# Second softmax five groups ahead, a fixed deviation bound and row-tiled up products in an attention-then-MLP kernel

## The chip, the cores and the metric

The kernel runs on one NeuronCore of a Trainium2 chip. Its engines work side by side: PE multiplies matrices into PSUM, DVE (VectorE) and ACT (ScalarE) compute on SBUF and PSUM, POOL (GpSimd) computes on SBUF, and SP issues the DMAs. Each engine takes its instructions in a fixed order and waits on semaphores. The metric is the device time of one execution in microseconds (us), the median of several runs; lower is better.

## The reference

Four batches of 12480 tokens with 128 channels go through two attentions over 32 learned points, and the result goes through an MLP with squared ReLU. Cut to what matters:

```python
B, N, m, C = (4, 12480, 32, 128)            # w_in: 128 x 2048, w_out: 2048 x 128
def mab(q, kv):
    s = scale * (q @ kv.transpose(0, 2, 1))
    s = s - s.max(-1, keepdims=True)
    a = np.exp(s)
    a /= a.sum(-1, keepdims=True) + 1e-09
    return a @ kv
h = mab(I, x)                               # (B, 32, C): the first softmax, over the tokens
y = mab(x, h)                               # (B, N, C): the second softmax, over the 32 points
r = np.maximum(y @ w_in, 0.0)
out = (r * r) @ w_out
```

## The kernel before

**What is computed.** A token's second softmax has 32 weights a, which sum to one and are all near 1/32. So y @ w_in = a @ (h @ w_in), and for nearly all of the 2048 hidden columns the sign is the same for every token of a batch. A column that is always positive contributes a quadratic form in a; one that is always negative contributes nothing; up to 16 columns a batch may change their sign and are computed one by one. The kernel stores d = 2^14 (a - 1/32) as two f16 halves, high and low.

**Stages of a batch.** `first(b)` computes h: for each of seven groups G of 1920 tokens (the last has 960) it loads the transposed tokens into a tile `xp` (L231), multiplies them with the points (`scores`, L236), keeps the scaled scores `sT` and their maxima (L254), then takes exponentials (L300), transposes them (L310) and sums `hacc` over the tokens, which come through five `xnb` buffers (L267, L323). Along the way `largest(G)` reduces the whole `xp` tile on DVE to its largest absolute value per channel, `xm` (L292). At the end stands the transposed h, `hT`. `prepare(b)` turns h and the weights into the matrices of the quadratic form: `hwv` (L448), the maximum and the bound in `row` (L473 to L482), `R`, `rb`, `cat`, then four times a product `G` on DVE (L605) and its matmul `wq` (L611) into `w16`. The bound `rho` on how far a token can lie from the mean of the 32 points is worked out here from `xm` and `hT` (`dh`, `ah`), and `vm`, `up`, `dn` decide with it which columns keep their sign. `second(b, G)` makes the scores against h from the same `xp` tile (L236), the softmax (L362 to L378) with two steps on POOL (L368, L375), the halves `a16` (L385 to L388), writes them to DRAM (`ad`, L389) and reads them back in another layout (`dT`, `load_dT`, L409: rows 0-31 high halves, 32-63 low halves, 64-95 high halves again). `squares(b, G)` multiplies `dT` for the single columns (`sq`, L422), cuts at zero (L428), squares on POOL (L432) and copies the result by DMA into rows 96-127 of `dT` (L434).

**The MLP.** A group has four chunks of 480 tokens, a batch 26, the whole kernel 104. For a chunk, `up(j)` makes two blocks of differences of weights by two matmuls of 96 rows (L639) with the constant matrix `pairs`, whose rows 64-95 are zero, into two PSUM banks; `lift(j)` squares both blocks on ACT (L648); `down` sums four blocks with `w16` (L654) and the row with `lin` (L655), and the output `o` leaves PSUM on ACT (L658) or DVE (L660), whichever has the smaller tally in `held`, and is stored (L661).

**What sets the order.** The loop at the end of the function emits lifts, ups and downs of neighbouring chunks and calls `background(k)` after each half chunk. It hands out steps of three generators: `ahead` (all `second`), `sqs` (all `squares`) and `nexts[b]` (`first` and `prepare` of the next batch), each up to a count that grows with the chunk. A scheduler then places the emitted instructions on the engines by its own timing model, so the order of a row on an engine may differ from that of the text. `dT` has 4 buffers, `xp` has `NX` = 9 (a batch's seven and two of the next), `g`, the lifted blocks, 3 and `o` 3. All DMAs shown are issued by SP, one after the other. At the end a flag for each batch is combined, and if one is zero, a slow general branch computes everything again; with the drawn inputs it is not taken.

Of the kernel before, what the change touches and what calls it, by code (L numbers as in the profile page):

```python
# [9 lines left out]
F32 = mybir.dt.float32  # L10
F16 = mybir.dt.float16
# [17 lines left out]
BLK = [(w + 31) // 32 for w in WID]  # L29
NQ = 4  # L30
MX = 16
RHO_MAX = 2.0 ** -8
NX = 9
XB = 5
RUNS = [(0, 4), (4, 4), (8, 4), (12, 4)]
BESIDE = (3, 2)
WHEN = (0, 2, 4, 8, 10, 12, 14)


@with_exitstack  # L40
def attend_then_relu2_mlp(ctx: ExitStack, tc: tile.TileContext, xn, xT, indT, w_in, w_out, outT):
# [64 lines left out]
    pairs = const.tile([P, NQ * P], F16, name="pairs")  # L106
    nc.vector.memset(pairs, 0.0)
    fold_f = fold.rearrange("p k i -> p (k i)")
    for s in range(1, 17):
        n = MI if s < 16 else 16  # L110
        nc.vector.tensor_tensor(
            pairs[0:64, MI * (s - 1):MI * (s - 1) + n], fold_f[0:64, 0:n], fold_f[0:64, s:s + n], op=ALU.subtract,
        )
    nc.vector.tensor_copy(pairs[0:64, 31 * 16:32 * 16], fold_f[0:64, 0:16])

    w_in_sb = const.tile([P, NF * P], F32, name="w_in_sb")
    wo_sb = const.tile([P, NF, P], F32, name="wo_sb")
# [122 lines left out]
    def first(b):  # L240
# [46 lines left out]
        nc.vector.tensor_scalar(nb, bp[:, 0:1], -1.0, None, op0=ALU.mult)  # L287
        yield

        def largest(G):  # L290
            held["dve"] += 60 + 1.042 * 4 * WID[G]
            nc.vector.tensor_reduce(  # L292
                st.xm[:, G:G + 1], st.xp[G], axis=AX.X, op=ALU.max, apply_absolute_value=True,
            )
# [12 lines left out]
        for G, nb32 in enumerate(BLK):  # L307
            en = work.tile([P, 15, MI], F32, tag="en", name=f"en_{b}_{G}")
            held["dve"] += 110 + 1.042 * 32 * nb32
            nc.vector.transpose(  # L310
                en[:, 0:nb32].rearrange("p t i -> p (t i)"), sT[:, 480 * G:480 * G + 32 * nb32],
            )
            if G + 2 < NG:
                exp(G + 2)
            largest(G)
            yield
            hacc = att_psum(f"hacc_{b}_{G}")
            for t in range(nb32):
# [4 lines left out]
                st.last = nc.tensor.matmul(  # L323
                    hacc[32 * q:32 * q + 32, 0:P], en[:, t], xg[:, t % 8], start=t < 4, stop=t + 4 >= nb32,
                )
# [23 lines left out]
    def second(b, G, again=False):  # L349
# [38 lines left out]
            nc.vector.scalar_tensor_tensor(a16[:, 1, 0:w], a[:, 0:w], lessen, a16[:, 0, 0:w], op0=ALU.add, op1=ALU.subtract)  # L388
# [15 lines left out]
    def load_dT(b, G):  # L404

        w = GRP[G] * TP
        dT = mlp.tile([P, 4, 480], F16, tag="dT", name=f"dT_{b}_{G}", bufs=4)
        for k in range(3):
            nc.sync.dma_start(  # L409
                dT[32 * k:32 * k + 32, :, 0:w], sts[b].ad[:, :, k % 2, 480 * G:480 * G + w].rearrange("q i n -> i q n"),  # L410
            )
        return dT
# [24 lines left out]
    def prepare(b):  # L437
# [6 lines left out]
        for h in range(2):  # L444
# [7 lines left out]
            if h == 0:

                xm, dh, ah = small("xm"), small("dh", MI), small("ah", MI)
                nc.vector.tensor_reduce(xm, st.xm, axis=AX.X, op=ALU.max)
                ts(dh, st.hT[:, 0:MI], st.hT[:, P:P + 1], None, op0=ALU.subtract)
                stt(dh, dh, -1.0, dh, op0=ALU.mult, op1=ALU.max)
                stt(ah, st.hT[:, 0:MI], -1.0, st.hT[:, 0:MI], op0=ALU.mult, op1=ALU.max)
                stt(dh, ah, 2.0 ** -18, dh, op0=ALU.mult, op1=ALU.add)
# [15 lines left out]
        row = work.tile([1, 2], F32, tag="row", name=f"row_{b}")
        nc.vector.tensor_reduce(row[:, 0:1], ps[0:1, 0:P], axis=AX.X, op=ALU.max)
        nc.vector.tensor_reduce(row[:, 1:2], ps[0:1, P:P + MI], axis=AX.X, op=ALU.max)
        ts(row[:, 0:1], row[:, 0:1], 2.0 ** -60, None, op0=ALU.max)
        ts(row[:, 1:2], row[:, 1:2], 2 * scale * (1 + 2.0 ** -8), 2.0 ** -16, op0=ALU.mult, op1=ALU.add)
        yield  # L480
        ps = att_psum(f"bc_{b}")
        nc.tensor.matmul(ps[:, 0:2], ones, row, start=True, stop=True)  # L482
        two = small("two", 2)
        nc.vector.tensor_copy(two, ps[:, 0:2])
        rho = two[:, 1:2]
# [60 lines left out]
        fits = work.tile([1, 2], F32, tag="fits", name=f"fits_{b}")  # L546
        ts(fits[:, 0:1], bp[0:1, 2:3], MX + 0.5, None, op0=ALU.is_le)
        ts(fits[:, 1:2], row[:, 1:2], RHO_MAX, None, op0=ALU.is_le)
        tt(flags[:, b:b + 1], fits[:, 0:1], fits[:, 1:2], op=ALU.mult)
# [79 lines left out]
    class Chunk:  # L629
# [4 lines left out]
        def up(self, j):  # L634
            if j == 0:
                self.dT = self.st.aT[self.c // 4][:, :, (self.c % 4) * TP:(self.c % 4 + 1) * TP]
            hp = self.hp[j] = two_banks(f"hp_{self.b}_{self.c}_{j}")
            for i in range(2):
                nc.tensor.matmul(  # L639
                    hp[:, i, 0:CH].rearrange("p (q t) -> p q t", q=4), pairs[0:96, (2 * j + i) * P:(2 * j + i + 1) * P],  # L640
                    self.dT[0:96], start=True, stop=True,
                )

        def lift(self, j):
# [59 lines left out]
    ahead = chain(*(second(b, G) for b in range(NB) for G in range(NG)))  # L704
# [235 lines left out]
```

## Time and profile before

| | us |
|---|---|
| three runs | 562.49, 556.12, 562.29 |
| their median | 562.29 |
| the profiled execution | 565.03 |
| its span, first to last instruction | 563.2 |

The profile is of one further execution; its mean granted TensorE clock is 0.87 of full speed. In the profile a row of the timeline gives start, length, engine, line, operation, tiles and count, and in brackets how long the engine had been idle before it and what ended that. This is the page's view of the span in 40 equal slices of 14 us, in tenths (9 is 90% or more): PE's busy share, and the clock that PE was granted.

```profile
PE   1635355986778988869789889779779989669792
PEclk9999557699697998776899988878898999898987
```

The first eight slices hold the start and the first batch's preparation; the MLP runs from there to the end.

### The profile page before, as it was taken

To read this page: it belongs to the slowest core of one execution; us is meant where nothing else is said; L and a number is where in the kernel's file an instruction comes from. 1 tells how busy PE (TensorE), PEld (TensorE's weight loads), DVE (VectorE), ACT (ScalarE), POOL (GpSimd) and SP (SyncE) were. 2 spreads that over 40 slices of the span, in tenths; PEclk is the share of its full clock that TensorE was granted. 3 is DMA by queue.
4 is the path that set the end of the run, shared out by engine and by line. 5 is a ranking of instruction groups with operands and counts; after the bars stand their busy time and mean duration, and the time that the engine had idled before them with its cause. 6 is when DMAs were issued, how large, how long until landed. Compare 5 with 4: busy or idle time off the path is not lost.

```text
span 563.2 us, 8828 instructions
## 1 busy us (share of the span) xinstructions
PE 422.6 (75%) x3083; PEld 202.7 (36%) x3083; DVE 365.6 (65%) x947; ACT 294.4 (52%) x419; POOL 82.2 (15%) x93
## 2 busy tenths in 40 slices
PE   1635355986778988869789889779779989669792
PEld 0023334622233535522244536423234555223340
DVE  8999768466382674675574384986653377787541
ACT  0030113338395794334687883426486875357771
POOL 0000011021120110122211010132121021234200
PEclk9999557699697998776899988878898999898987
DMA  8998313126559863253778943263567312244642
GB/s 317 410 358 310 132 70 118 41 80 212 140 160 345 292 216 115 72 169 107 216 237 294 334 167 115 76 227 115 174 216 264 128 54 72 90 151 133 203 150 82
DMA packets 64591, 100.83 MB, mean 179 GB/s; under 512 B 22800, under 2 KB 53776, under 8 KB 64528
## 3 DMA queue, kind: packets, MB, share of 16 engines
q1 hardware_dynamic: 64528, 100.08, 52.9%
q8 instruction: 28, 0.46, 0.4%
q14 instruction: 35, 0.29, 0.2%
HBM read 64.91 MB, written 31.95 MB: 172 GB/s over the span
## 4 chain that ended last, share of the span: by engine, by line
PE 39%; DMA 24%; DVE 22%; ACT 5%; SPq 4%; issue 3%; POOL 0%; ACTq 0%; DVEq 0%; POOLq 0%
PE hp L639 11%; DMA dT<-ad 7%; PE po L654 6%; PE s L236 6%; DMA xp_False<-xT_dram 6%; DMA ad<-a 5%; DVE xm L292 5%; ACT g L648 4%; DMA xnb<-xn_dram 3%; PE wq L611 3%; DVE G L605 3%; PE hwv L448 3%; PE hacc L323 2%; SPq L409 2%; DMA outT_dram<-o 2%
## 5 line engine op out<-in xcount | busy, mean ns | idle before, releaser
L648 ACT ACTIVATE g<-hp 128x960 f16<-128x960 f32 x208 | 193.5, 972 | 105.0 <-PE hp L639 92.8
L639 PE MATMUL hp<-dT,pairs 96*128 96x480 f16 x416 | 129.3, 407 | 16.2 <-ACT g L648 9.6
L654 PE MATMUL po<-g,w 128*128 128x480 f16 x416 | 114.7, 381 | 13.0 <-DVE o L660 5.1
L639 PEld LDWEIGHTS <-pairs 96*128 96x128 f16 x416 | 36.8, 104 | 84.4 <-issue 60.2
L368 POOL TENSOR_TENSOR e<-e,mx 128x480 f32<-128x480 f32 (+1 forms) x28 | 27.0, 965 | 261.5 <-DVE mx L364 208.2
L654 PEld LDWEIGHTS <-w 128*128 128x128 f16 x416 | 40.9, 102 | 63.6 <-issue 24.6
L292 DVE TENSOR_REDUCE xm<-xp_False 128x1 f32<-128x1920 f32 (+1 forms) x28 | 55.9, 1999 | 8.4 <-DMA xp_False<-xT_dram 8.3
L658 ACT ACTIVATE o<-po,bias,osc 128x480 f32<-128x480 f32 x66 | 48.7, 757 | 15.6 <-PE po L655 14.7
L236 PE MATMUL s<-xp_False,indT_sb 128*32 128x480 f32 (+1 forms) x224 | 37.4, 756 | 18.3 <-DMA xp_False<-xT_dram 13.3
L323 PE MATMUL hacc<-xnb,en 128*32 128x128 f32 x784 | 35.6, 317 | 19.6 <-DMA xnb<-xn_dram 7.6
L655 PE MATMUL po<-dT,lin 128*128 128x480 f16 x104 | 39.9, 400 | 9.3 <-DMA dT<-zz 9.0
L432 POOL TENSOR_TENSOR zz<-z 128x480 f16<-128x480 f32 (+1 forms) x28 | 27.6, 985 | 111.7 <-DVE z L428 87.9
L660 DVE TENSOR_SCALAR o<-po,osc,bias 128x480 f32<-128x480 f32 x38 | 28.8, 763 | 18.4 <-PE po L655 13.7
L375 POOL TENSOR_TENSOR e<-e,z 128x480 f32<-128x480 f32 (+1 forms) x28 | 26.9, 961 | 87.8 <-DVE z L374 67.6
L323 PEld LDWEIGHTS hacc<-xnb,en 128*32 128x32 f32 x784 | 25.5, 125 | 32.5 <-issue 15.7
L300 ACT ACTIVATE sT<-sT,nb 128x480 f32<-128x480 f32 (+1 forms) x28 | 18.3, 657 | 35.2 <-DVE nb L287 35.2
L362 DVE STREAM_TRANSPOSE e<-s 128x480 f32<-128x480 f32 (+1 forms) x28 | 18.0, 644 | 25.6 <-PE s L236 25.4
L428 DVE TENSOR_SCALAR z<-sq,off,cut 128x480 f32<-128x480 f32 (+1 forms) x28 | 21.5, 769 | 18.0 <-PE sq L422 17.5
L236 PE MATMUL s<-xp_False,hT 128*32 128x480 f32 (+1 forms) x224 | 30.0, 610 | 0.1
L605 DVE TENSOR_TENSOR G<-hwp,hw 128x512 f16<-128x512 f16 x64 | 25.9, 460 | 5.6 <-PE wq L611 5.6
L378 DVE STREAM_TRANSPOSE a<-e 128x480 f32<-128x480 f32 (+1 forms) x28 | 17.7, 633 | 13.0 <-POOL e L375 13.0
L422 PE MATMUL sq<-dT,singles 96*32 96x480 f16 x104 | 11.4, 398 | 19.4 <-DMA dT<-ad 18.0
(208 smaller groups left out, 493.3 us busy)
## 6 DMA issues: line engine op xcount, KB each, us to landing
outT_dram<-o SPq DMA_DIRECT2D x104, 240.0 KB, 2.6
xp_False<-xT_dram SPq DMA_DIRECT2D x24, 960.0 KB, 6.3
xnb<-xn_dram SPq DMA_DIRECT2D x28, 448.0 KB, 5.8
xnb<-xn_dram SPq DMA_DIRECT2D x24, 512.0 KB, 6.5
dT<-ad SPq DMA_DIRECT2D x72, 120.0 KB, 2.6
ad<-a SPq DMA_DIRECT2D x24, 240.0 KB, 2.6
dT<-zz SPq DMA_DIRECT2D x104, 30.0 KB, 1.9
wi<-w_in_dram SPq DMA_DIRECT2D x4, 512.0 KB, 5.7
```

Source lines behind the costliest of these rows:

```text
L236: nc.tensor.matmul(ps[32 * q:32 * q + 32, 0:w], lhsT, xp[:, w * q:w * q + w], start=True, stop=True,)
L292: nc.vector.tensor_reduce(st.xm[:, G:G + 1], st.xp[G], axis=AX.X, op=ALU.max, apply_absolute_value=True,)
L323: st.last = nc.tensor.matmul(hacc[32 * q:32 * q + 32, 0:P], en[:, t], xg[:, t % 8], start=t < 4, stop=t + 4 >= nb32,)
L368: nc.gpsimd.tensor_tensor(e[:, 0:t], e[:, 0:t], mx[:, 0:t].unsqueeze(2).broadcast_to([P, t, MI]), op=ALU.subtract)
L432: nc.gpsimd.tensor_tensor(g[rows], zv[rows], zv[rows], op=ALU.mult)
L605: tt(g[:, :, MI * j:MI * j + n], hwp[:, :, 0:n], hw16f[:, :, s0:s0 + n], op=ALU.mult)
L639: nc.tensor.matmul(hp[:, i, 0:CH].rearrange("p (q t) -> p q t", q=4), pairs[0:96, (2 * j + i) * P:(2 * j + i + 1) * P], self.dT[0:96], sta ...
L648: nc.scalar.activation(self.g[:, 2 * j:2 * j + 2], self.hp.pop(j)[:, 0:2, 0:CH], AF.Square)
L654: nc.tensor.matmul(po[:, 0:CH], st.w16[:, i], self.g[:, i], start=i == 0, stop=False)
L655: nc.tensor.matmul(po[:, 0:CH].rearrange("p (q t) -> p q t", q=4), st.lin, self.dT, start=False, stop=True)
L658: nc.scalar.activation(o, po[:, 0:CH], AF.Identity, bias=st.bias, scale=st.osc)
L660: nc.vector.tensor_scalar(o, po[:, 0:CH], st.osc, st.bias, op0=ALU.mult, op1=ALU.add)
```

## The change

It has six parts, all in the one function.

1. **Fixed bound.** `rho` becomes the constant 2^-10. `xm`, `largest`, `dh`, `ah`, the second column of `row` and the check of `rho` go. In their place `second` keeps the smallest high half of d so far in `least_d`, and a new generator `smallest`, behind the last `second`, compares it with -0.498 into a further flag.
2. **Row-tiled up products.** The matrix `pairs` stands in rows 0-31 for even blocks and in rows 64-95 for odd ones, and an up product reads those 32 rows of `pairs` and of `dT`, which hold high halves in both places. The low halves are left out of the up products.
3. `ahead` runs up to five groups ahead (was three), not into a batch whose h isn't made yet; `dT` has six buffers.
4. `sqs` runs up to two groups ahead (was one).
5. The next batch's steps are handed out earlier: scores by chunk 6 (was 8), heads by 12 (was 15), `prepare` by 22 (was 24.5); they are handed out before `ahead`.
6. `NX` is 8 (was 9).

```diff
-RHO_MAX = 2.0 ** -8
-NX = 9
+RHO = 2.0 ** -10
+D_MIN = -0.498
+NX = 8
+NDT = 6
...
+    def half_rows(block):
+        return slice(64, 96) if block % 2 else slice(0, 32)
...
+        r = half_rows((s - 1) // 4)
         nc.vector.tensor_tensor(
-            pairs[0:64, MI * (s - 1):MI * (s - 1) + n], fold_f[0:64, 0:n], fold_f[0:64, s:s + n], op=ALU.subtract,
+            pairs[r, MI * (s - 1):MI * (s - 1) + n], fold_f[r, 0:n], fold_f[r, s:s + n], op=ALU.subtract,
...
-        def largest(G):
-            held["dve"] += 60 + 1.042 * 4 * WID[G]
-            nc.vector.tensor_reduce(
-                st.xm[:, G:G + 1], st.xp[G], axis=AX.X, op=ALU.max, apply_absolute_value=True,
-            )
...
-            largest(G)
...
         if not again:
+            nc.vector.tensor_tensor(least_d[:, 0:w], least_d[:, 0:w], a16[:, 0, 0:w], op=ALU.min)
             st.aT[G] = load_dT(b, G)
...
-        dT = mlp.tile([P, 4, 480], F16, tag="dT", name=f"dT_{b}_{G}", bufs=4)
+        dT = mlp.tile([P, 4, 480], F16, tag="dT", name=f"dT_{b}_{G}", bufs=NDT)
...
-        nc.tensor.matmul(ps[0:1, P:P + MI], xm, dh, start=True, stop=True)
...
-        ts(vm, v, omr, None, op0=ALU.mult)
-        ts(up, hi, 0.0, rho, op0=ALU.max, op1=ALU.mult)
+        ts(vm, v, 1.0 - RHO, None, op0=ALU.mult)
+        ts(up, hi, 0.0, RHO, op0=ALU.max, op1=ALU.mult)
...
+                r = half_rows(i)
                 nc.tensor.matmul(
-                    hp[:, i, 0:CH].rearrange("p (q t) -> p q t", q=4), pairs[0:96, (2 * j + i) * P:(2 * j + i + 1) * P],
-                    self.dT[0:96], start=True, stop=True,
+                    hp[:, i, 0:CH].rearrange("p (q t) -> p q t", q=4), pairs[r, (2 * j + i) * P:(2 * j + i + 1) * P],
+                    self.dT[r], start=True, stop=True,
...
-        give("ahead", ahead, min(math.ceil((NG * b + c / 4 + min(3, 2 + k / 16)) * N_SECOND), NB * NG * N_SECOND))
...
-            if c < 8:
-                want = 1 + N_SCORES * c / 8
-            elif c < 15:
-                want = 1 + N_SCORES + N_HEADS * (c - 8) / 7
+            if c < 6:
+                want = 1 + N_SCORES * c / 6
+            elif c < 12:
+                want = 1 + N_SCORES + N_HEADS * (c - 6) / 6
             else:
-                want = 1 + N_SCORES + N_HEADS + N_PRE * (c - 15) / 9.5
+                want = 1 + N_SCORES + N_HEADS + N_PRE * (c - 12) / 10
             give(b + 1, nexts[b + 1], math.ceil(want))
-        give("sqs", sqs, min(math.ceil(NG * b + c / 4 + 1), NG * (b + 1)) * N_SQ)
+        known = NB if b + 1 == NB else b + 1 + (c >= 12)
+        far = math.ceil((NG * b + c / 4 + min(5, 3 + k / 8)) * N_SECOND)
+        give("ahead", ahead, min(far, NG * known * N_SECOND) + (far > NB * NG * N_SECOND))
+        give("sqs", sqs, min(math.ceil(NG * b + c / 4 + min(2, 1 + k / 8)), NG * (b + 1)) * N_SQ)
```

How the instructions move is seen on the engines themselves. The first place is SP's queue where batch 1 begins. Names end in batch, group or chunk and a running number: `ad_154<-a_1_2` is the write of batch 1's third group, `dT_2` its way back, `zz_0` the squares of the first group, `o_0` the first chunk's output. Before:

```order
L434 DMA dT_0_1914<-zz_0_2170 32x4x120 x4
L434 DMA dT_1_2128<-zz_1_2252 32x4x120 x4
L661 DMA outT_dram<-o_0_2275 128x480
L661 DMA outT_dram<-o_1_2303 128x480
L231 DMA xp_6_False<-xT_dram 128x960
L661 DMA outT_dram<-o_2_2334 128x480
L661 DMA outT_dram<-o_3_2368 128x480
L389 DMA ad_154<-a_1_2_2203 256x1x480
L409 DMA dT_2_2207<-ad_154 32x4x480 x3
L389 DMA ad_154<-a_1_3_2339 256x1x480
```

And now:

```order
L391 DMA ad_154<-a_1_2_2028 256x1x480
L412 DMA dT_2_2033<-ad_154 32x4x480 x3
L240 DMA xp_4_False<-xT_dram 128x1920
L240 DMA xp_5_False<-xT_dram 128x1920
L437 DMA dT_0_1560<-zz_0_2183 32x4x120 x4
L437 DMA dT_1_1809<-zz_1_2237 32x4x120 x4
L437 DMA dT_2_2033<-zz_2_2281 32x4x120
L391 DMA ad_154<-a_1_3_2136 256x1x480
L437 DMA dT_2_2033<-zz_2_2281 32x4x120 x3
L412 DMA dT_3_2141<-ad_154 32x4x480 x3
L647 DMA outT_dram<-o_0_2308 128x480
```

The third group's write and way back moved from behind the fourth output to before the first; the fourth group's came up behind it, and three groups of squares stand in a row instead of two.

The second place is ACT at the same boundary: `g` are lifts (two a chunk, from `hp`), `w_1` the copies of batch 1's four weight matrices out of `wq`, which its downs need. Before:

```order
L648 ACTIVATE g_1_2264<-hp_1_0_2218 128x960
L648 ACTIVATE g_1_2264<-hp_1_1_2259 128x960
L165 ACTIVATE w_1_146<-wq_0_1928,tsg 128x128
L648 ACTIVATE g_2_2292<-hp_2_0_2266 128x960
L648 ACTIVATE g_2_2292<-hp_2_1_2287 128x960
L165 ACTIVATE w_1_146<-wq_1_1975,tsg 128x128
L369 ACTIVATE e_1_1_1971<-e_1_1_1971 128x480
L165 ACTIVATE w_1_146<-wq_2_2028,tsg 128x128
```

And now:

```order
L634 ACTIVATE g_2_2325<-hp_2_0_2299 128x960
L634 ACTIVATE g_2_2325<-hp_2_1_2316 128x960
L371 ACTIVATE e_1_2_1860<-e_1_2_1860 128x480
L174 ACTIVATE w_1_146<-wq_0_1877,tsg 128x128
L644 ACTIVATE o_24_2200<-po_24_2194,bias_143,osc_142 128x480
L174 ACTIVATE w_1_146<-wq_1_1921,tsg 128x128
L387 ACTIVATE a_1_2_2028<-a_1_2_2026,lessen 128x480
L174 ACTIVATE w_1_146<-wq_2_1968,tsg 128x128
```

The weight copies did not move up: all four stand behind the lifts of the new batch's third chunk now, while the softmax exponential beside them is one group further on.

The third place is DVE while batch 1's weights are made (`G` feeds `wq`, `wm` reads it). Before:

```order
L605 TENSOR_TENSOR G_2_2007<-hwp_1745,hw_1_1697 128x16x32 x4
L428 TENSOR_SCALAR z_6_1997<-sq_6_1994,off_137,cut 64x480
L613 TENSOR_REDUCE wm_1918<-wq_1_1975 128x1
L372 TENSOR_REDUCE z_1_1_2071<-e_1_1_1971 128x15
L292 TENSOR_REDUCE xm_133<-xp_3_False 128x1
L373 TENSOR_SCALAR z_1_1_2071<-z_1_1_2071 128x15
L605 TENSOR_TENSOR G_3_2051<-hwp_1745,hw_1_1697 128x16x32 x3
```

And now:

```order
L590 TENSOR_TENSOR G_2_1954<-hwp_1680,hw_1_1644 128x16x32 x4
L646 TENSOR_SCALAR o_25_2254<-po_25_2248,osc_142,bias_143 128x480
L598 TENSOR_REDUCE wm_1849<-wq_1_1921 128x1
L390 SCALAR_TENSOR_TENSOR a_1_2_2028<-a_1_2_2026,lessen,a_1_2_2028 128x480
L393 TENSOR_TENSOR least_d<-least_d,a_1_2_2028 128x480
L590 TENSOR_TENSOR G_3_1987<-hwp_1680,hw_1_1644 128x16x32 x3
```

The reduction of a whole `xp` tile ahead of the last `G` is gone; an output, the low half and the new minimum stand there. Over the whole kernel 61 outputs are on DVE now instead of 38.

More of the change, by code (lines that the diff above doesn't have):

```diff
@@ L108, in attend_then_relu2_mlp @@
     fold_f = fold.rearrange("p k i -> p (k i)")
+    def half_rows(block):
+        return slice(64, 96) if block % 2 else slice(0, 32)
     for s in range(1, 17):
         n = MI if s < 16 else 16
+        r = half_rows((s - 1) // 4)
         nc.vector.tensor_tensor(
-            pairs[0:64, MI * (s - 1):MI * (s - 1) + n], fold_f[0:64, 0:n], fold_f[0:64, s:s + n], op=ALU.subtract,
+            pairs[r, MI * (s - 1):MI * (s - 1) + n], fold_f[r, 0:n], fold_f[r, s:s + n], op=ALU.subtract,
         )
-    nc.vector.tensor_copy(pairs[0:64, 31 * 16:32 * 16], fold_f[0:64, 0:16])
+    r = half_rows(NQ - 1)
+    nc.vector.tensor_copy(pairs[r, 31 * 16:32 * 16], fold_f[r, 0:16])
     w_in_sb = const.tile([P, NF * P], F32, name="w_in_sb")
@@ L119, in attend_then_relu2_mlp @@
     inv_t = const.tile([P, 1], F32, name="inv_t")
-    flags = const.tile([1, NB], F32, name="flags")
+    flags = const.tile([1, NB + 1], F32, name="flags")
+    least_d = const.tile([P, CH], F16, name="least_d")
+    nc.vector.memset(least_d, 0.0)
     class Batch:
@@ L127, in attend_then_relu2_mlp @@
         one = Batch()
-        one.xm = const.tile([P, NG], F32, name=f"xm{k}")
         one.hn = const.tile([P, P], F32, name=f"hn{k}")
@@ L451, in prepare @@
             evac(hwv[:, 8 * h:8 * h + 8].rearrange("p k i -> p (k i)"), ps[:, 0:8 * (MI + 1)], 8 * (MI + 1))
[L452 to L459, printed above, removed]
             yield
@@ L473, in prepare @@
         nc.tensor.transpose(ps[0:1, 0:P], am, ident)
-        nc.tensor.matmul(ps[0:1, P:P + MI], xm, dh, start=True, stop=True)
[L475 to L479, printed above, removed]
+        row = work.tile([1, 1], F32, tag="row", name=f"row_{b}")
+        nc.vector.tensor_reduce(row, ps[0:1, 0:P], axis=AX.X, op=ALU.max)
+        ts(row, row, 2.0 ** -60, None, op0=ALU.max)
         yield
         ps = att_psum(f"bc_{b}")
[L482 to L485, printed above, removed]
+        nc.tensor.matmul(ps[:, 0:1], ones, row, start=True, stop=True)
         p2 = small("p2")
-        ts(p2.bitcast(I32), two[:, 0:1].bitcast(I32), 0x7F800000, None, op0=ALU.bitwise_and)
-        mg, nmg, s, k2, omr = small("mg"), small("nmg"), small("s"), small("k2"), small("omr")
+        ts(p2.bitcast(I32), ps[:, 0:1].bitcast(I32), 0x7F800000, None, op0=ALU.bitwise_and)
+        mg, nmg, s, k2 = small("mg"), small("nmg"), small("s"), small("k2")
         ts(k2, p2, 2.0, None, op0=ALU.mult)
@@ L500, in prepare @@
         ts(nmg, p2, -2.0 ** -16, None, op0=ALU.mult)
-        ts(omr, rho, -1.0, 1.0, op0=ALU.mult, op1=ALU.add)
         up, dn, dead, pos, mix, inc = (small(n, NF) for n in ("up_c", "dn_c", "dead", "pos", "mix", "inc"))
         vm = small("vm", NF)
-        ts(vm, v, omr, None, op0=ALU.mult)
-        ts(up, hi, 0.0, rho, op0=ALU.max, op1=ALU.mult)
+        ts(vm, v, 1.0 - RHO, None, op0=ALU.mult)
+        ts(up, hi, 0.0, RHO, op0=ALU.max, op1=ALU.mult)
         tt(up, up, vm, op=ALU.add)
@@ L508, in prepare @@
         stt(dead, up, nmg, dead, op0=ALU.is_le, op1=ALU.max)
-        ts(dn, lo, 0.0, rho, op0=ALU.min, op1=ALU.mult)
+        ts(dn, lo, 0.0, RHO, op0=ALU.min, op1=ALU.mult)
         tt(dn, dn, vm, op=ALU.add)
@@ L545, in prepare @@
         stt(inc, inc, pl, mix, op0=ALU.add, op1=ALU.mult)
[L546 to L549, printed above, removed]
+        ts(flags[:, b:b + 1], bp[0:1, 2:3], MX + 0.5, None, op0=ALU.is_le)
         hot = flow.tile([P, NF, MX], F32, tag="hot", name=f"hot_{b}", bufs=1)
@@ L703, in attend_then_relu2_mlp, with smallest @@
     N_SECOND, N_SCORES, N_HEADS, N_PRE, N_SQ = 4, 2 * NG, 20, 23, 2
-    ahead = chain(*(second(b, G) for b in range(NB) for G in range(NG)))
+    def smallest():
+        m = small("dmin")
+        nc.vector.tensor_reduce(m, least_d, axis=AX.X, op=ALU.min)
+        tp = att_psum("dmin_t")
+        nc.tensor.transpose(tp[0:1, 0:P], m, ident)
+        t = work.tile([1, 1], F32, tag="dmin1", name="dmin1")
+        nc.vector.tensor_reduce(t, tp[0:1, 0:P], axis=AX.X, op=ALU.min)
+        nc.vector.tensor_scalar(flags[:, NB:NB + 1], t, D_MIN, None, op0=ALU.is_ge)
+        yield
+    ahead = chain(*(second(b, G) for b in range(NB) for G in range(NG)), smallest())
     sqs = chain(*(squares(b, G) for b in range(NB) for G in range(NG)))
```

## The prediction, made before the changed kernel was run

> **What bounds the kernel now.** I read the page first, for the engines and the chain that ended last, then the span cut into stages (cut where the chain shows one batch's steps end), then PE's waits by what ended them, and last the timeline at the places that the change touches. The page, busy time and then the chain by line:
>
> ```profile
> PE 422.6 (75%) x3083; PEld 202.7 (36%) x3083; DVE 365.6 (65%) x947; ACT 294.4 (52%) x419; POOL 82.2 (15%) x93
> PE hp L639 11%; DMA dT<-ad 7%; PE po L654 6%; PE s L236 6%; DMA xp_False<-xT_dram 6%; DMA ad<-a 5%; DVE xm L292 5%; ACT g L648 4%; DMA xnb<-xn_dram 3%; PE wq L611 3%; DVE G L605 3%; PE hwv L448 3%; PE hacc L323 2%; SPq L409 2%; DMA outT_dram<-o 2%
> ```
>
> No engine is full. The chain changes hands all the time: PE, the trip of the second softmax's result through DRAM (ad, then dT), and the DVE reductions xm. So the stages matter (start and end in us, busy time of PE, PEld, DVE, ACT and POOL, granted clock, DMA share):
>
> ```profile
> core 0: us, PE busy (x) PEld busy (x) DVE busy (x) ACT busy (x) POOL busy (x), PEclk, DMA share, GB/s
> 0.00:65.00 65.00, 24.87 (x258) 11.06 (x258) 62.04 (x149) 5.95 (x15) 1.18 (x9) 0.95 0.88 331
> 65.00:116.00 51.00, 35.52 (x236) 24.65 (x236) 30.58 (x110) 13.86 (x21) 3.97 (x4) 0.63 0.20 63
> 116.00:171.00 55.00, 39.82 (x283) 13.92 (x283) 33.55 (x67) 37.26 (x58) 11.81 (x12) 0.90 0.52 162
> 171.00:191.00 20.00, 18.70 (x182) 8.98 (x182) 8.67 (x27) 13.25 (x17) 2.22 (x3) 0.84 1.02 356
> 191.00:245.00 54.00, 45.45 (x302) 26.47 (x303) 33.84 (x106) 29.33 (x42) 5.89 (x6) 0.82 0.43 139
> 245.00:293.00 48.00, 37.33 (x228) 12.01 (x227) 31.33 (x63) 28.63 (x45) 11.20 (x11) 0.85 0.58 185
> 293.00:320.00 27.00, 24.63 (x257) 12.68 (x257) 13.88 (x39) 22.40 (x31) 3.21 (x4) 0.94 0.93 309
> 320.00:367.00 47.00, 39.60 (x291) 23.75 (x291) 32.10 (x104) 25.34 (x37) 6.10 (x6) 0.87 0.40 138
> 367.00:412.00 45.00, 37.23 (x199) 11.69 (x198) 33.09 (x70) 22.19 (x30) 10.95 (x11) 0.83 0.56 178
> 412.00:441.00 29.00, 24.37 (x277) 11.76 (x275) 12.14 (x35) 23.09 (x38) 3.17 (x4) 0.94 0.70 229
> 441.00:483.00 42.00, 36.73 (x297) 22.77 (x296) 29.16 (x103) 27.23 (x39) 5.91 (x6) 0.98 0.22 70
> 483.00:563.00 80.00, 58.40 (x289) 22.96 (x286) 45.23 (x83) 45.88 (x53) 16.61 (x17) 0.91 0.44 141
> ```
>
> Row 1 is the start (first softmax of batch 0, weights narrowed): DVE is busy 62 of 65 us, the DMA engines 88%. Row 2 is `prepare` of batch 0. Then each batch has three stages: the batch's head, where the second softmax has to get ahead of the MLP (116, 245, 367); the sums `hacc` of the next batch (171, 293, 412); its `prepare` (191, 320, 441). The last row is the last batch alone. In the heads PE idles 15.2, 10.7 and 7.8 us, and its clock is 0.90, 0.85 and 0.83; in the last row 21.6 us at 0.91. What ended PE's waits, with total, times and longest:
>
> ```profile
> PE sq L422 <- DMA dT<-ad: 18.0, 7, 4.4
> PE po L655 <- DMA dT<-zz: 9.0, 5, 1.9
> PE hp L639 <- DMA dT<-ad: 6.3, 5, 2.0
> ```
>
> PE stands on dT for 24.3 us, and pays again after it: here the same 8 score matmuls take 1.01 us before an idle stretch of 3.36 us and 1.84 us after it.
>
> ```profile
> 249.97 1.01 PE L236 MATMUL s<-xp_False,indT_sb 128*32 128x480 f32 x8 [0.30 <-DVE z L428]
> 254.34 0.59 PE L422 MATMUL sq<-dT,singles 96*32 96x480 f16 x4 [3.36 <-DMA dT<-ad]
> 254.69 1.84 PE L236 MATMUL s<-xp_False,indT_sb 128*32 128x480 f32 x8
> ```
>
> [...]
>
> **The change part by part.** The profiled execution took 565.0 us with a span of 563.2; the median of the three runs shown is 562.3, 2.7 lower. The sum is made against 565.0 and then lowered by 2.7.
>
> *Start.* The 28 reductions xm go. By stage (DVE busy, count, clock, DMA share, GB/s of that line):
>
> ```profile
> 0.00:65.00 65.00, 18.20 (x9) 0.95 0.88 331
> 65.00:116.00 51.00, 4.30 (x2) 0.63 0.20 63
> 191.00:245.00 54.00, 6.23 (x3) 0.82 0.43 139
> 320.00:367.00 47.00, 4.28 (x2) 0.87 0.40 138
> sum 563.00, DVE 55.90; mean DVE 4.66
> ```
>
> Nine of them, 18.2 us, lie in the start, where DVE has 3 us of slack: 65 - 18.2 = 46.8 us would be DVE's end. But the DMA engines are the next bound: 0.88 x 65 = 57.2 us, less one xp tile (0.98 MB at 331 GB/s, 3.0 us), which the order now puts behind the last xn tile: 54 us. So -11 (ends: -14, if the DMA engines pack better, and -5, if their idle stretches stay).
>
> *`prepare` of batch 0.* Two xm, 4.3 us, one of them ahead of the first reductions of hwv; the bound row (xm, dh, ah, rho and its matmul), about ten DVE operations of a column or two, goes as well. Nothing is put in. I take -4 (-2 to -6, the upper end being both xm and the small ones).
>
> *Second softmax five groups ahead, six dT buffers.* In the order, the dT load of a batch's third group now stands before that batch's first output instead of behind its fourth, and later groups stand 7 to 16 chunks ahead of their first use instead of 3 to 8. The first group of a batch stays where it was, about four chunks ahead. That takes the direct waits, 24.3 us, and part of the slow clock: in the three heads and the last stage the clock loses 5.5 + 7.2 + 7.7 + 7.2 = 27.6 us ((1 - clock) x length). I take half of that, 13.8: -38 in all. Ends: -52 (all of both) and -12 (half the direct waits, if another wait stands behind them). DVE is late next: 31 to 34 us busy in heads of 45 to 55.
>
> *Squares two ahead, next batch sooner.* The squares of a batch's sixth and seventh group stand directly before their use in both orders, so the 9.0 us of PE on zz mostly stay. The next batch's last weight matmuls stand where they stood, after four chunks of the new batch's lifts. I take 0 for both. A new cost: at a batch's begin SP now has twelve zz issues in a row instead of eight, with the ad of the fourth group and the first outputs behind. Eight took
>
> ```profile
> 251.26 8.10 SPq L434 DMA_DIRECT2D dT<-zz  x8
> ```
>
> so 4 more are 4 us of SP, three times; they are covered as long as the fourth group's dT, now 9 to 12 chunks ahead, isn't due. If that cover goes, +12 at most.
>
> *DVE and ACT in the MLP.* The balance moves 23 of the 66 outputs o from ACT to DVE, and each of the 28 groups gets a minimum over 128x480 f16.
>
> ```profile
> L658 ACT ACTIVATE o<-po,bias,osc 128x480 f32<-128x480 f32 x66 | 48.7, 757 | 15.6 <-PE po L655 14.7 <-ACT o L658 0.7 <-ACT g L648 0.2
> L660 DVE TENSOR_SCALAR o<-po,osc,bias 128x480 f32<-128x480 f32 x38 | 28.8, 763 | 18.4 <-PE po L655 13.7 <-DMA outT_dram<-o 4.6
> L605 DVE TENSOR_TENSOR G<-hwp,hw 128x512 f16<-128x512 f16 x60 | 25.1, 473 | 5.6 <-PE wq L611 5.6
> L388 DVE SCALAR_TENSOR_TENSOR a<-a,lessen,a 128x480 f16<-128x480 f32 x24 | 18.0, 754 | 3.9 <-ACT a L385 3.7
> ```
>
> DVE: 55.9 - 18.2 - 4.3 = 33.4 us of xm go; 23 x 0.763 = 17.5 come, and 28 minima at 0.44 (473 ns x 480/512, the nearest row in type) are 12.4, at 0.754 they would be 21. DVE's sum hardly moves (-3.5, or +5); ACT loses 17.4, but is not the bound in any stage. What counts is the place: five xm, 10.5 us, stand between the serial steps of the later `prepare`s, and the minima stand behind the ad issue's data, off that path. I take -9 (0, if outputs fall into the same gaps, to -13).
>
> *Row-tiled up products.* Two products on rows 0-31 and 64-95 can run together: a pair streams for 0.205 us instead of 0.41 (two hp in 0.42, two po in 0.40, below), 208 x 0.205 = 42.6 us of PE at full clock. But PE now changes between whole-array and tiled products at every pair. No row-tiled product is in the trace; the column-tiled ones (sq, hacc) are nearest:
>
> ```profile
> 183.01 0.36 PE L655 MATMUL po<-dT,lin 128*128 128x480 f16 x1
> 183.31 0.39 PE L422 MATMUL sq<-dT,singles 96*32 96x480 f16 x4
> 183.52 0.61 PE L323 MATMUL hacc<-xnb,en 128*32 128x128 f32 x16
> ...
> 187.04 0.58 PE L639 MATMUL hp<-dT,pairs 96*128 96x480 f16 x2
> 187.46 0.57 PE L654 MATMUL po<-g,w 128*128 128x480 f16 x2
> 187.86 0.57 PE L639 MATMUL hp<-dT,pairs 96*128 96x480 f16 x2
> ```
>
> ```profile
> 306.79 0.39 PE L422 MATMUL sq<-dT,singles 96*32 96x480 f16 x4
> 307.11 0.58 PE L639 MATMUL hp<-dT,pairs 96*128 96x480 f16 x2
> ```
>
> Into tiling: one po, then sq after 0.30 instead of 0.20, so 0.10 us. Out of it: hp 0.32 after sq, where tiled hacc comes 0.21 after, so 0.11 us. Counted over PE's order up to the last up product there are 448 such changes instead of 189: 259 more x 0.105 = 27 us. Net -15 us of PE. PE is the bound for about half of the time (the `hacc` stages and the full stretches), so -8. Ends: -32 (no price for a change; 42.6 x PE's 75%) and +9 (a change at 0.2, a whole stream).
>
> [...]
>
> The sum: -11 - 4 - 38 - 9 - 8 = -70; 565.0 - 70 = 495; less 2.7, **492 us**. The fallback branch stays untaken: in the drawn inputs the smallest deviation, worked out from the reference, is -0.064, against a limit of -0.498.
>
> **The rivals.** *Tiling for free:* a change to row tiling costs nothing; 492 - 24 = 468. For it: the rows' prices are for column tiling. Against: 0.10 and 0.11 appear at each change I looked at. *The wait moves:* PE no longer stands on dT but on the new batch's weights, since lifts run four chunks ahead and `prepare` ends where it ended; the third term is -12, so 518. For it: `prepare` stages of 42 to 54 us with DVE only 60 to 70% busy are a chain of steps, not a full engine. *The lookahead doesn't act:* dT comes earlier in the order only, since its groups wait on DVE or SP; terms three and four are 0, so 539. Against: PE's waits name the DMA. *Slower:* each change of mode waits out a whole pass (0.36 us for one product, row at 183.01) and the pair doesn't run together: 259 x 0.36 = 93 us in place of -8, so 492 + 8 + 93 = 593. It decides from 0.28 us a change without overlap, 0.45 with it: then the other -62 are eaten and 11 more. Against: 0.10 and 0.11. [...] *Hardly any change:* all terms at their poor ends, -5 - 2 - 12 + 0 + 9 = -10, so 552.
>
> **How the numbers follow.** Chances: the sum 0.40, tiling for free 0.18, the wait moves 0.22, the lookahead doesn't act 0.09, hardly any change 0.05, slower 0.06. About 2% (11 us) is what a measurement of this kernel can tell from no change. Faster is the first four, 0.89; same 0.05; slower 0.06. The predicted time is the likeliest, 492, whose own range is 475 to 512. The range for all, 455 to 535, holds it and both neighbours, 468 and 518, 0.80 together; it leaves out 539 and beyond.
>
> **What would show it.** Start: hT's batch-0 transposition ends near 53 instead of 64 us. dT: the waits of sq and hp on dT fall from 24.3 to under 8 us, and the heads' clock rises above 0.9. Tiling: hp to po in about 0.30 to 0.32 (0.20 if free), and PE busy falls by some 15 to 20 us, not 60. `prepare`: the stretch from hwv to the last wq shrinks by about 3 us a batch, not more. DVE's busy time falls by 25 to 35 us. I am wrong if a head is as long as now with PE waiting on something else, or if the pair's second product starts only after the first.

## The result and the profile after

| | us | ratio to before, 95% interval |
|---|---|---|
| after, first comparison (before: 562.39) | 527.69 | 0.932 [0.918, 0.946] |
| after, once more in a later set of runs (before: 558.37) | 527.15 | 0.946 [0.939, 0.952] |
| the profiled execution of after (span 523.3) | 525.1 | |

The change gains 31 to 35 us by the medians, half of the 70 that were forecast. The medians take in all runs and the ratios only each kernel's fast ones, without two of the four of after (530.28 and 531.23 us); the profiles of two kernels below, after with whole rows and xn early, are of slow runs. The page of after, busy time and chain by line:

```profile
PE 400.5 (77%) x3076; PEld 176.6 (34%) x3076; DVE 333.9 (64%) x936; ACT 279.3 (53%) x390; POOL 82.2 (16%) x93
PE po L640 11%; DMA xnb<-xn_dram 7%; ACT g L634 6%; PE hp L625 6%; PE s L245 6%; DMA dT<-zz 5%; PE hacc L325 4%; PE hwv L451 3%; DMA wo<-w_out_dram 3%; DMA ad<-a 3%; DVE G L590 3%; PE po L641 3%; PE wq L596 3%; PE R L517 2%; DMA dT<-ad 2%
```

PE is 22 us less busy and DVE 32, but xm's place in the chain went to xnb and zz. By stage (columns as before; rows 1 and 2 start and `prepare` of batch 0, then head, `hacc`, `prepare` for each further batch, then the last batch):

```profile
0.00:54.00 54.00, 26.04 (x263) 12.00 (x263) 47.19 (x142) 5.94 (x15) 1.18 (x9) 0.78 0.98 372
54.00:97.00 43.00, 31.08 (x231) 21.96 (x231) 25.96 (x98) 13.69 (x20) 4.18 (x4) 0.66 0.26 85
97.00:144.00 47.00, 36.99 (x254) 11.46 (x255) 28.32 (x65) 34.65 (x53) 12.72 (x13) 0.94 0.64 201
144.00:167.00 23.00, 19.98 (x236) 9.89 (x227) 9.14 (x27) 18.52 (x27) 1.60 (x2) 0.95 0.96 306
167.00:216.00 49.00, 39.08 (x301) 21.17 (x301) 31.27 (x106) 27.63 (x41) 8.28 (x8) 0.90 0.55 181
216.00:248.00 32.00, 25.15 (x178) 7.92 (x178) 25.61 (x66) 20.79 (x31) 10.93 (x12) 1.00 0.73 227
248.00:282.00 34.00, 27.31 (x280) 11.54 (x278) 10.69 (x29) 21.05 (x30) 0.99 (x1) 0.85 0.84 286
282.00:335.00 53.00, 43.75 (x315) 22.62 (x314) 37.08 (x116) 26.35 (x36) 7.80 (x8) 0.84 0.41 136
335.00:372.00 37.00, 31.56 (x200) 9.18 (x198) 29.60 (x71) 21.99 (x27) 11.40 (x12) 0.91 0.65 201
372.00:401.00 29.00, 24.20 (x265) 10.21 (x264) 9.28 (x26) 20.62 (x34) 0.98 (x1) 0.82 0.62 214
401.00:453.00 52.00, 42.38 (x307) 22.91 (x306) 37.31 (x115) 23.55 (x32) 8.05 (x8) 0.84 0.23 76
453.00:524.00 71.00, 52.99 (x272) 15.70 (x272) 42.41 (x80) 44.48 (x51) 14.05 (x15) 0.86 0.44 140
```

Start -11, `prepare` of batch 0 -8, the heads -8, -16 and -8, the last batch -9; but `hacc` +3, +7, 0 and the later `prepare`s -5, +6, +10. PE's waits for DMAs are no shorter than before (dT 24.3, zz 9.0, xp 13.3, xnb 7.6: 54 us), only for other things: 61 us.

```profile
PE po L641 <- DMA dT<-zz: 22.5, 9, 3.8
PE hacc L325 <- DMA xnb<-xn_dram: 17.3, 14, 3.8
PE s L245 <- DMA xp_False<-xT_dram: 17.0, 7, 11.4
...
PE hp L625 <- DMA dT<-ad: 4.0, 4, 3.1
```

A comparison by stage can't say which part of the change did this, since a wait that leaves one stage may come back in another. So parts were run alone.

### The profile page after: what moved, and what is told of

Read it like the earlier page. It is cut to its first block, busy times and chain, and to the rows that moved or that the text cites. A ratio compares the mean times of both kernels' runs of the same rounds, so it can differ in the third digit from the quotient of the medians.

```text
span 523.3 us, 8758 instructions
## 1 busy us (share of the span) xinstructions
PE 400.5 (77%) x3076; PEld 176.6 (34%) x3076; DVE 333.9 (64%) x936; ACT 279.3 (53%) x390; POOL 82.2 (16%) x93
## 4 chain that ended last, share of the span: by engine, by line
PE 41%; DMA 23%; DVE 17%; ACT 9%; issue 5%; POOL 1%; SPq 1%; ACTq 0%; POOLq 0%; DVEq 0%
PE po L640 11%; DMA xnb<-xn_dram 7%; ACT g L634 6%; PE hp L625 6%; PE s L245 6%; DMA dT<-zz 5%; PE hacc L325 4%; PE hwv L451 3%; DMA wo<-w_out_dram 3%; DMA ad<-a 3%; DVE G L590 3%; PE po L641 3%; PE wq L596 3%; PE R L517 2%; DMA dT<-ad 2%
## 5 line engine op out<-in xcount | busy, mean ns | idle before, releaser
L640 PE MATMUL po<-g,w 128*128 128x480 f16 x416 | 123.8, 401 | 10.3 <-DVE o L646 4.1
L625 PE MATMUL hp<-dT,pairs 32*128 32x480 f16 x416 | 82.1, 391 | 12.3 <-ACT g L634 7.7
L646 DVE TENSOR_SCALAR o<-po,osc,bias 128x480 f32<-128x480 f32 x61 | 47.0, 773 | 26.8 <-PE po L641 19.1
L641 PE MATMUL po<-dT,lin 128*128 128x480 f16 x104 | 42.6, 420 | 22.6 <-DMA dT<-zz 22.5
L325 PE MATMUL hacc<-xnb,en 128*32 128x128 f32 x784 | 39.8, 336 | 23.1 <-DMA xnb<-xn_dram 17.3
L640 PEld LDWEIGHTS <-w 128*128 128x128 f16 x416 | 31.4, 101 | 70.7 <-issue 51.1
L625 PEld LDWEIGHTS <-pairs 32*128 32x128 f16 x416 | 21.4, 94 | 80.2 <-issue 73.4
L644 ACT ACTIVATE o<-po,bias,osc 128x480 f32<-128x480 f32 x43 | 32.1, 756 | 22.5 <-PE po L641 13.9
L371 ACT ACTIVATE e<-e 128x480 f32<-128x480 f32 (+1 forms) x28 | 16.1, 577 | 25.6 <-POOL e L370 25.5
L596 PEld LDWEIGHTS <-G 128*128 128x128 f16 x256 | 19.2, 116 | 22.7 <-DVE wm L598 6.7
L596 PE MATMUL wq<-w_hi,G 128*128 128x128 f16 x256 | 21.8, 254 | 6.1 <-DVE G L592 3.5
L517 PE MATMUL R<-wo_sb,hwS 128*32 128x128 f32 x128 | 21.5, 348 | 6.3 <-DVE hwS L508 6.3
```

Source lines behind the costliest of these rows:

```text
L325: st.last = nc.tensor.matmul(hacc[32 * q:32 * q + 32, 0:P], en[:, t], xg[:, t % 8], start=t < 4, stop=t + 4 >= nb32,)
L517: nc.tensor.matmul(ps[0:MI, 0:P], hwS[:, k], wo_sb[:, k], start=k == 0, stop=k == NF - 1)
L596: nc.tensor.matmul(ps[:, 0:P], g[:, k], w_hi[:, k], start=k == 0, stop=k == NF - 1)
L625: nc.tensor.matmul(hp[:, i, 0:CH].rearrange("p (q t) -> p q t", q=4), pairs[r, (2 * j + i) * P:(2 * j + i + 1) * P], self.dT[r], start=Tru ...
L640: nc.tensor.matmul(po[:, 0:CH], st.w16[:, i], self.g[:, i], start=i == 0, stop=False)
L641: nc.tensor.matmul(po[:, 0:CH].rearrange("p (q t) -> p q t", q=4), st.lin, self.dT, start=False, stop=True)
```

## The experiments

The runs were taken in three sets, each on one chip beside its own runs of the kernel before (555.19, 558.37 and 555.32 us). Ratios are to that, with 95% intervals.

**1. The fixed bound alone** (before, with the first part of the change's diff only).

> The kernel before with the fixed bound alone (xm gone, one minimum per group; the lookahead, paces, buffers and up products of before). The prediction's terms: start -11, prepare of batch 0 -4, the later prepares -3 each: 538 to 540. Rival, that the outputs which the balance moves to DVE fill the gaps: start and prepare of batch 0 as said, the later prepares (54, 47 and 42 us before) no shorter: 545 to 548.

524.96 us, 0.944 [0.935, 0.953]: -31, more than either theory. hwv of batch 0 starts at 56.4 us (67.2 before), its `prepare` takes 45.8 us (48.5), and every stretch from hwv to the next hwv (or the end) is 4 to 9 us shorter. This part alone is worth nearly what the whole change is worth. The later `prepare`s are not where it comes from: from hwv to the last wq they take 45.2, 51.4 and 44.7 us (54.1, 47.3 and 42.1 before), 2 less in all. Of the 37 us that the profiled span loses, 21 lie between a batch's last wq and the next hwv or the end, for which the prediction had no term for this part. PE's waits on dT are 7.8 us there (24.3 before), with the lookahead as it was, so the two parts shorten in part the same wait:

```profile
PE sq L425 <- DMA dT<-ad: 5.3, 7, 1.5
PE hp L624 <- DMA dT<-ad: 2.5, 5, 1.0
```

It depends on the order, too: with row tiling added (experiment 3) or fillers (experiment 6) these waits are 16.9 us. Why the stretches behind the `prepare`s shrink was not tested.

**2. The lookahead alone.**

```diff
-NX = 9
+NX = 8
-dT = mlp.tile([P, 4, 480], F16, tag="dT", name=f"dT_{b}_{G}", bufs=4)
+dT = mlp.tile([P, 4, 480], F16, tag="dT", name=f"dT_{b}_{G}", bufs=6)
-give("ahead", ahead, min(math.ceil((NG * b + c / 4 + min(3, 2 + k / 16)) * N_SECOND), NB * NG * N_SECOND))
+known = NB if b + 1 == NB else b + 1 + (c >= 15)
+give("ahead", ahead, min(math.ceil((NG * b + c / 4 + min(5, 3 + k / 8)) * N_SECOND), NG * known * N_SECOND))
```

> The kernel before with the second softmax five groups ahead, six dT buffers and eight xp buffers alone. The prediction's third term: -38, 524, heads and last batch shorter by 30 to 40 in all. Rival, the wait moves: -12, 550. Third reading, from the trace of after: the heads shrink by about 35 but the prepares grow by about 10, since second-softmax work now stands beside them: 535 to 540.

546.77 us, 0.984 [0.975, 0.993]: 9 us, not 38. PE's waits for DMAs in this run, and those of wq for G:

```profile
PE hacc L323 <- DMA xnb<-xn_dram: 14.4, 8, 4.4
PE s L236 <- DMA xp_False<-xT_dram: 14.2, 4, 12.0
PE wq L611 <- DVE G L607: 9.6, 4, 3.0
PE po L655 <- DMA dT<-zz: 9.3, 5, 4.4
...
PE sq L422 <- DMA dT<-ad: 6.7, 3, 5.3
...
PE wq L611 <- DVE G L605: 4.5, 4, 2.4
...
PE hp L639 <- DMA dT<-ad: 0.3, 1, 0.3
```

dT fell from 24.3 to 7.0 us, as meant; but xnb rose by 6.8, and PE's waits for G, from which the new batch's weights are made, from 1.3 to 14.1 (for all of DVE from 52.7 to 58.6). zz stayed (9.0 before). The second and third head are 8 and 9 us shorter, the last batch 12, but the first head is 3 longer and the three later `prepare`s are 2, 9 and 7.

**3. Row tiling taken back, and put on the fixed bound alone.** The first has up products over rows 0 to 95, both halves; the second is experiment 1 with 32-row products, high halves only.

```diff
-    hp[:, i, 0:CH].rearrange("p (q t) -> p q t", q=4), pairs[r, (2 * j + i) * P:(2 * j + i + 1) * P],
-    self.dT[r], start=True, stop=True,
+    hp[:, i, 0:CH].rearrange("p (q t) -> p q t", q=4), pairs[0:96, (2 * j + i) * P:(2 * j + i + 1) * P],
+    self.dT[0:96], start=True, stop=True,
```

> The changed kernel with its up products over rows 0 to 95 again (high and low halves, as before the change). The prediction's price of a change of tiling (0.10 in, 0.11 out) with 42.6 us of streams saved: 8 us slower than the changed kernel, about 535, PE busy up by 15 to 22. Rival, tiling for free: 24 to 32 slower, 550 to 560. Rival from the trace of after, where a lone pair takes 0.41 us with or without tiling: 0 to 4 slower, 527 to 532, since only the runs of four up products gain.

> The kernel before with the fixed bound and the row-tiled up products, the lookahead, paces and buffers as before. If the bound (-30) and the tiling (-8 by the prediction's price) are nearly all of the change: 0.92 to 0.935, no slower than the changed kernel, and the lookahead is worth nothing on top. If the lookahead is worth the prediction's third term beside them: 30 us slower than the changed kernel, about 0.98. If tiling gains nothing and the lookahead 8: 0.945.

> The changed kernel once more, beside the other three of this call: about 0.93 of the kernel before. With whole rows at 0.953 it would give row tiling 2%, some 12 us; nearer 0.95 would give it nothing.

530.85 us, 0.953 [0.943, 0.964], against 0.932 and 0.946 for after; and 534.46 us, 0.953 [0.945, 0.960], against 0.944 for the bound alone. Taken back it costs up to 2%, added it costs 1%: nothing that shows. The two products of a pair do run together: in the trace of after the second starts 4 ns behind the first (median at full clock; 206 ns before). Each pair is as forecast, 0.31 us to the next product, and 0.51 from two po back to hp, where they take 0.40 alone. So a lone pair, with whole-array products on both sides, still costs 0.42, what two hp took before:

```profile
505.30 0.37 PE L625 MATMUL hp<-dT,pairs 32*128 32x480 f16 x2
505.61 0.58 PE L640 MATMUL po<-g,w 128*128 128x480 f16 x2
506.12 0.38 PE L625 MATMUL hp<-dT,pairs 32*128 32x480 f16 x2
```

**4. The next batch's pace as before** (scores to chunk 8, heads to 15, `prepare` from there), run twice.

> The changed kernel with the pace of the next batch as before (scores over 8 chunks, heads to 15, prepare over the rest), all else as changed. The prediction gave this part 0: 525 to 531. If the sooner pace is what lengthens the prepare stages: 515 to 520 and prepares of 42 to 47 again. If the sooner pace is what shortens the heads: 540 or more.

> The changed kernel with the next batch's pace as before, once more, on this chip: 0.935 to 0.945 of the kernel before. If its earlier 0.939 was the chip's or the windows' chance, it falls together with the changed kernel.

521.30 us, 0.939 [0.928, 0.950], and 525.91 us, 0.944 [0.937, 0.950]: no different from after, as forecast. Yet PE's waits on zz and xnb, 22.5 and 17.3 us in after, are 8.6 and 9.8 here (8.4 and 9.3 the second time). So these two waits can shrink without the time following:

```profile
PE hacc L325 <- DMA xnb<-xn_dram: 9.8, 9, 3.3
PE po L641 <- DMA dT<-zz: 8.6, 5, 4.5
```

**5. The waits that came up, taken on directly.** Squares three groups ahead, those of the next batch's first two groups from the step on that makes its singles (`READY`); and the next batch's first five xn tiles loaded behind the last `hacc` of the batch (the third line of the second diff).

```diff
+soon = 2 if b + 1 < NB and given[b + 1] >= READY else 0
-give("sqs", sqs, min(math.ceil(NG * b + c / 4 + min(2, 1 + k / 8)), NG * (b + 1)) * N_SQ)
+give("sqs", sqs, min(math.ceil(NG * b + c / 4 + min(3, 1 + k / 8)), NG * (b + 1) + soon) * N_SQ)
```
```diff
-xns = {h: load_xn(h) for h in range(XB)}
+xns = st.xns if b else {h: load_xn(b, h) for h in range(XB)}
+sts[b + 1].xns = {h: load_xn(b + 1, h) for h in range(XB)}
```

> The changed kernel with the squares three groups ahead, and those of the next batch's first two groups given as soon as that batch's singles are there. PE's waits on zz (22.5 us in the changed kernel) fall under 8. If they are on the path: 10 to 15 us faster than the changed kernel. If prepare's serial chain ends the batch anyway: within 4 us of it, with the idle time moved to wq and R.

> The changed kernel with the first five xn tiles of the next batch loaded when the batch's own sums are done, not behind its scores. PE's waits on xnb (17.3 us) fall under 8 and the hacc stages (20 to 25 us) to 13 to 17. If they are on the path: 10 to 15 us faster than the changed kernel. If the MLP chunks that run beside hacc set the length: within 4 us.

542.41 us, 0.968 [0.959, 0.977], and 539.40 us, 0.959 [0.951, 0.967]: both slower than after, and both miss their aim (zz 18.5, xnb 14.2 us). PE's idle time is that of after (123 and 121 us, after 123 and 125). What grew in the profiles is time at half clock, which led to the next experiment. For xn early the size isn't shown: its profile is of the longest of five runs (547.23 us, clock 0.81), and three of the others had 0.84 to 0.85; all five of the squares had 0.79 to 0.82.

**PE's clock.** Here are five stretches of after, 3.41 us each, and three of an earlier place (columns as above):

```profile
197.53:200.94 3.41, 3.30 (x34) 2.01 (x36) 1.81 (x9) 2.21 (x3) 0.00 (x0) 1.00 0.00 0
200.94:204.36 3.42, 3.16 (x32) 1.50 (x25) 3.03 (x11) 2.24 (x3) 0.81 (x1) 1.00 0.48 133
204.36:207.77 3.41, 0.27 (x3) 0.17 (x3) 2.46 (x8) 0.86 (x2) 1.12 (x2) 1.00 0.47 180
207.77:211.18 3.41, 3.05 (x22) 1.91 (x21) 2.29 (x6) 1.70 (x3) 0.99 (x1) 0.50 0.22 77
211.18:214.59 3.41, 2.21 (x24) 1.28 (x25) 3.33 (x10) 0.37 (x1) 0.00 (x0) 1.00 0.39 144
```

```profile
163.39:166.81 3.42, 3.42 (x20) 1.76 (x20) 1.22 (x6) 3.42 (x6) 0.00 (x0) 1.00 0.94 317
166.81:170.22 3.41, 3.41 (x33) 3.37 (x34) 0.00 (x0) 0.88 (x2) 0.00 (x0) 1.00 1.05 305
170.22:173.63 3.41, 3.41 (x16) 0.57 (x15) 2.06 (x12) 2.21 (x3) 0.00 (x0) 0.50 0.92 343
```

PE idles from 204 to 207 us, and the whole next window is at 0.50; behind a window that is 89% busy it is 1.00 again. In the second place the hwv products (33 columns each, PEld 3.37) fill a window, and still the next is at half. In each of the 14 profiles all changes of the clock lie on one raster of 3.413 us, to within 0.05 us, whose offset differs between executions (2.97 us here, 0.88 in the bound alone). Over all profiles, from 110 us on, all 122 windows at full clock with PE under 45% busy are followed by one at half, and all 104 at half with PE under 80% busy by another at half. Between 50 and 65% the clock falls behind 4 of 33 windows of the five kernels with whole-row up products, and behind 37 of 86 of the nine row-tiled ones. Of 856 windows with PE over 80% busy at full clock, only 25 are followed by one at half: 22 of them hold 21 to 32 of the hwv products, the other three 22 to 34 of rb. PE's time, in busy time times clock (A), the rest of the busy time (B), and idle time (C), in us. The record shows no half clock before 58 us in before and 23 in after, though eight score products took 1.83 us at 12.34 us in before and 1.01 at 249.97; by half the time of such rows B lacks some 6 us in before, 5 in the bound alone and 3 in after (an estimate). Two profiles of one kernel differ in B by 3 us (after, 58 and 55) and by 7 (the next batch's pace as before, 56 and 63).

| | A | B, lost at half clock | C, idle | span |
|---|---|---|---|---|
| before | 369 | 54 | 141 | 563 |
| lookahead alone | 362 | 54 | 133 | 549 |
| fixed bound alone | 370 | 42 | 114 | 527 |
| fixed bound and row tiling | 344 | 71 | 119 | 533 |
| after | 343 | 58 | 123 | 523 |
| after with whole rows | 360 | 59 | 113 | 533 |
| squares three ahead | 341 | 76 | 123 | 540 |
| xn early | 342 | 82 | 121 | 545 |

**6. The clock held by filler** in batch 0's `prepare`, 40 products (4 ahead of ht, 8 among hwv, 10 ahead of am, 18 ahead of R), on after and on the bound alone.

```diff
+def warm(n, after):
+    with tc.issue_after(after.ins):
+        for i in range(n):
+            nc.tensor.matmul(idle[:, 0:CH], pairs[:, 0:P], pairs[:, 0:CH], start=True, stop=True)
```

> The changed kernel with 40 products of 128x480 that nothing reads put into PE's idle stretches of batch 0's prepare (4 ahead of ht, 8 among hwv, 10 ahead of am, 18 ahead of R). Theory: PE's clock is set window by window (3.41 us) by how busy PE was in the window before, so these hold it: the granted clock of 54 to 79 us rises from about 0.5 to above 0.9, R of batch 0 falls from 5.73 to about 3.7 us, two hwv halves from 3.36 and 3.62 to about 2.3 each with the fillers in them, prepare of batch 0 from 42 to 43 us down to 36 to 39; the time 3 to 7 lower than the changed kernel. Rival: the clock drops for another reason (its first row of fp32 products): R stays at 5 to 6 us and the fillers make the stretch longer.

> The kernel before with the fixed bound alone and the same 40 fillers in batch 0's prepare. If fillers and bound add: 3 to 7 below the bound alone (0.944), 0.931 to 0.939, as fast as or faster than the whole change. If the clock that is lost there comes back elsewhere: 0.944.

On after: 533.89 us, 0.962 [0.957, 0.967], slower than after; on the bound alone: 517.82 us, 0.931 [0.926, 0.937], lower than the bound's 0.944 [0.935, 0.953], though the intervals just overlap. In the first, the windows 54 to 79 and 79 to 98 us, and R:

```profile
54.00:79.00 25.00, 20.43 (x136) 12.24 (x136) 17.16 (x63) 9.70 (x14) 4.44 (x4) 0.93 0.37 128
79.00:98.00 19.00, 16.30 (x133) 11.33 (x131) 8.65 (x36) 3.66 (x7) 0.00 (x0) 0.55 0.11 33
```

```profile
73.24 3.68 PE L531 MATMUL R<-wo_sb,hwS 128*32 128x128 f32 x32
```

The theory of the clock holds in the filled stretch: 0.93 where after has 0.52, and R takes 3.68 us, not 5.73. But the half clock then falls on the second part (0.55; after 0.83), where the wq products stand, and `prepare` takes 44.5 us, no less. With the bound alone it is the same (0.93, then 0.56; `prepare` 46.6 us, 45.8 without fillers), so what that kernel gained lies elsewhere. The fillers also change the order of later work: by the traces some 50 of 936 rows on DVE stand in another place than in after, and some 280 of 941 on the bound alone. The two kernels went opposite ways by 1 to 3%. The new order may have done this; it was not isolated.

**7. The outputs kept on ACT**, by the charge that went with xm.

```diff
 if G + 2 < NG:
     exp(G + 2)
+held["dve"] += 60 + 1.042 * 4 * WID[G]
```

> The changed kernel with the planner's charge for the removed xm kept, so that the outputs o stay on ACT as before (about 66 there, 38 on DVE, in place of 43 and 61). The prediction's fourth term says that DVE freed in the later prepares shortens them by 3 each. If the 23 outputs that moved to DVE are what took that back: prepares of batches 1 to 3 fall from 49 to 56 to 45 to 50 and the time by 6 to 10. If not: within 4 us.

509.11 us, 0.916 [0.911, 0.922]: 2 to 3% below after (0.932, 0.946), and the fastest of all; experiment 4's second run, of the same set, took 525.91. 69 outputs stand on ACT and 35 on DVE (after 43 and 61), DVE is busy 317.2 us (after 333.9). The later `prepare`s take 50.4, 47.4 and 47.8 us, hwv to last wq (after 48.8, 52.4, 51.3, and 48.6, 55.8, 51.3 the second time), and zz holds PE for less (after 22.5 us):

```profile
PE po L642 <- DMA dT<-zz: 8.7, 4, 3.4
```

A part of it may be the new order, as in experiment 6, and experiment 4 lost the wait on zz without a gain; that the outputs were all of it is not shown. Outputs on ACT with the fixed bound alone were not tried.

## Why the prediction held, and where it failed

Faster was right. That the time lies in the range of 455 to 535 owes to its width: it is outside the sum's own range (475 to 512), between the rivals "the wait moves" (518) and "the lookahead doesn't act" (539). Most signs that I had named came true (hT at 52.4 us, dT 4.0 us, the heads' clock 0.94, 1.00 and 0.91, hp to po 0.31, PE 22 and DVE 32 us less busy), and still the time didn't follow: they look at where a wait leaves, not at where it goes. The one that looks there failed: the later `prepare`s, hwv to last wq, did not shrink by 3 us each but went from 54.1, 47.3 and 42.1 to 48.8, 52.4 and 51.3.

- *Start, -11:* right (hwv of batch 0 at 53.9 and, with the bound alone, 56.4 us instead of 67.2).
- *`prepare` of batch 0, -4:* -3 with the bound alone, -5 with all parts (hwv to last wq, 48.5 before).
- *Second softmax and dT buffers, -38:* this step failed. Alone it gives 9 us. The direct waits went (24.3 to 7.0), but PE then waited for xnb (+6.8) and for G on DVE (+12.8); I had named DVE as late next, without a price. And the half of the clock loss (13.8), my estimate, is shown by no run: B is 54 us with and without the lookahead. The rival's -12 was about the right size, and its new wait, the weights of the new batch, was half of the truth: G is what they are made from. zz did not rise in this run; in after it did, but experiment 4 shows that it can fall again at no gain.
- *Squares and next batch, 0:* right for the pace. Twelve zz issues in a row weren't tested alone.
- *DVE and ACT, -9:* this did not come in after, where the later `prepare`s are together 9 us longer; with the bound alone they are 2 shorter. I had set 0 for the case that the outputs fall into the same gaps. Experiment 7 speaks for it: kept on ACT, the same kernel is 9 to 16 us faster by the ratios, though its later `prepare`s are still 2 us longer than before. What the bound gave outside the start and the `prepare`s, 21 us alone, stood in no term.
- *Row tiling, -8:* the prices 0.10 in and 0.11 out were right, and A falls by 18 (experiment 3's first) to 27 us (its second), more than the net 15. But in time it is 0: in the second pair B rises by 29 us. That goes with the windows between 50 and 65% busy, behind which the clock fell 37 times of 86 with row tiling and 4 of 33 without; that row tiling is the cause wasn't isolated.

Taken alone, the parts give -31 (bound), -9 (lookahead) and about 0; together -31 to -35. So the right direction rests mainly on the bound, which the sum gave -24, and the two errors, too little for it and too much for the lookahead, partly cancel.

## What to carry to other kernels

Run the parts of a change alone before crediting a stage: a wait removed in front of a shared engine is only worth what the next one leaves. When work is taken off an engine, look at what a balancing planner puts in its place; here the charge of the deleted work, kept, gave as much as the whole lookahead or more, though a new order may have a share in it. Price idle time of PE by whole clock windows (3.413 us in the 14 profiles here), not by its length.

## What was unexpected of the hardware

In the 14 profiles PE's clock changes on a raster of 3.413 us, whose offset is another in each (0.50 to 3.39 us). From 110 us on, behind a window at full clock and under 45% busy came half clock (122 of 122), behind one at half and under 80% busy half again (104 of 104), and of the 25 windows of 856 at full clock and over 80% busy that were followed by half clock 22 held 21 to 32 of the 33-column hwv products. In experiment 6, products that nothing reads held the clock at 0.93 in a stretch that was at 0.52, and R fell from 5.73 to 3.68 us; the half clock then came behind it (0.55 instead of 0.83).
